# Attention and two mixtures of experts: the test for spilled tokens moved between expert 0's two products, the second tile's loads and splits rearranged, and zero products added in the first steps

## The chip, the cores and the metric

The kernel runs on one core of one Trainium2 chip. Times are device microseconds (us) of one execution of the whole program, less is better. Three executions are timed and a further one is profiled. The engines are PE (TensorE, matmul; PEld is its loading of weights), DVE (VectorE), ACT (ScalarE), POOL (GpSimd) and SP (SyncE, which here issues transfers). A "q" behind an engine's name means its instruction queue, which issues transfers, waits on semaphores, loads registers and branches.

## The reference

Sliding-window attention gives the rows of x; a mixture that sends each token to one of 8 experts follows, and then one that weighs 4 experts for every token.

```python
# 1. attention: B, H, S, D = 4, 8, 576, 64; window of 128 keys, a bias by distance and head
scores = np.where(mask, scale * q @ k.T + bias, -1e9); attn = softmax(scores)
x = (attn @ v).transpose(0, 2, 1, 3).reshape(2304, 512)
# 2. each token to its best of 8 experts (512 -> 1024 -> 512)
expert_idx = np.argmax(x @ w_gate, axis=1)
for e in range(8):
    xe = x[expert_idx == e]
    out[expert_idx == e] = gate_w * (np.maximum(xe @ w1[e], 0.0) @ w2[e])
# 3. four experts for all tokens, weighted by p
out2 += p[:, e:e+1] * (np.maximum(out @ w1[e], 0.0) @ w2[e])
```

## The kernel before

The order of the work is the order of the code: every engine runs its own instructions in the order in which they are written, and waits on semaphores for the others.

**Attention** (`attention()`) goes over 18 tiles of 128 tokens, each in two half steps s (four heads each), so 36 steps. A step runs on PE the scores of step s (`st_qk`, tile sc: first the bias by an identity in bf16, then products of q and k, each split into a high and a low part: qhi, qlo, khi, klo), the product with v of step s - 2 (`st_pv`, xo), for every second step the product of v with the gate (`st_vw`, vw) and the transposes of the probabilities of step s - 1 (`st_pv_t`, pt). DVE takes the row maximum (`st_max`, nm), which ACT's exponentials wait for, and makes the splits of a later tile (`split_k`, `split_q`). Tiles 0 and 1 are loaded and split ahead of the loop.

**First mixture** (`first_mixture()`): the rows of x lie sorted by expert in device memory (xs), 2304 places per expert. For each expert e the first 384 rows (CH) are fetched (`fetch`, tile row), transposed on PE (tile xps) and split by ACT (xhi) and DVE (xlo). `unit1(e)` is two products: the first, tile g, in four pairs of hidden blocks of 24 matmuls; after each pair ACT and DVE make hhi and hlo of it (`hidden`), PE transposes a quarter of the next expert's rows (`nprep`), and one tile of weights is split (`w_split`: ACT whi, DVE wlo, then SP's issue of the weights two tiles on, into one of three buffers raw). The second product, tile y, follows in four groups of 24 matmuls. The matmuls stand in arms of `by_width`, chosen by the expert's count of tokens. `prep_first` does expert 0's transposes at once, all four tiles.

**The test.** An expert with more than 384 tokens spills: `spill(e)` holds a loop over further chunks of 128. All of it stands in one `tc.If(most > 0)`, where `most` is read by every engine from nov_i. So each engine's queue loads the number, compares and jumps over the code of eight experts' loops. Behind the jump it waits for its own work and adds to its semaphores what the code that was jumped would have added. A tile that the spilled code also uses is so released for the next user only when the engine concerned has passed the test: the PSUM tiles of `ps_a` (tag a), for one, which ACT reads in the spilled code and y uses after it.

Line 869 ff. hold 24 zero products on PE ("idle"), which no one reads, between attention and the first mixture; then come two `w_split`, the test, `prep_first`, the fetch of expert 1's rows, and the eight `unit1`.

Of the kernel before, what the change touches and what calls it, by code (L numbers as in the profile page):

```python
# [45 lines left out]
def kernel(  # L46
# [42 lines left out]
    const.tile([P, PAD], F32, tag="pad", name="pad")  # L89


    stream = [(w_a, e, j) for e in range(E1) for j in range(NW)]
# [33 lines left out]
    def attention():  # L126
        actx = ExitStack()
        with actx:
# [16 lines left out]

            def load(t):
                rk = rpool.tile([P, NP, P], F32, tag="rk", name=f"rk{t}")
                rq = rpool.tile([P, NP, P], F32, tag="rq", name=f"rq{t}")
                nc.sync.dma_start(out=rk, in_=k[t])
                nc.sync.dma_start(out=rq, in_=q[t])  # L150
                raw_q[t], raw_k[t] = rq, rk
# [30 lines left out]
            nc.vector.memset(zrow, 0.0)  # L182
            load(0)
            wgt = c2.tile([P, NDT, E1], F32, tag="wgt", name="wgt")
            nc.sync.dma_start(out=wgt, in_=wg)
            load_v(0)
            load(1)
            load_v(1)
# [35 lines left out]
            for h in range(H):  # L224
                build_bias(0, h, 0, 2 * P, nc.scalar)
            split_k(1)
            split_q(1)
            dpt = c2.tile([P, N // P, E2], F32, tag="dpt", name="dpt")
# [303 lines left out]
            for s in range(ns + 2):  # L532
                t, hf = divmod(s, 2)
                if s < ns:
                    st_qk(s)
                    st_max(s)
                    st_exp(s, 0)
# [47 lines left out]
    def moe():  # L585
        mctx = ExitStack()
        with mctx:
# [57 lines left out]
            def first_mixture():  # L645
                pctx = ExitStack()
                with pctx:
# [77 lines left out]
                    def unit1(e, nprep, extra):  # L725
# [9 lines left out]
                        for f0 in range(0, NFT, 2):  # L735
                            pair = [ps_g.tile([P, CH], F32, tag="g", name="g") for _ in range(2)]

                            def body(w):
                                for r, ps in enumerate(pair):
                                    g1(ps, x, w0, f0 + r, w)  # L740

                            by_width(wide, pair, body)
                            hidden(pair, hs)
                            nprep(f0 // 2)
                            w_split()
                            extra()
                        accs = [ps_a.tile([P, CH], F32, tag="a", name=f"y{e}_{dt}") for dt in range(NDT)]
                        if e == E1 - 1:
# [22 lines left out]

                    def spill(e):
                        cur = sp.tile([P, 1], F32, tag="cur", name=f"cur{e}")
# [6 lines left out]
                        with tc.For_i(0, chunks_e, 1):  # L780
                            spill_chunk(e, cur, to)

                    def spill_chunk(e, cur, to):
                        ok = sp.tile([P, 1], F32, tag="ok", name="ok")
# [20 lines left out]
                        nc.vector.tensor_copy(out=xt, in_=px)  # L805
                        ht = xp.tile([P, NFT, P], F32, tag="xhi", name="sht")
                        raw = xp.tile([P, F], F32, tag="xlo", name="sraw")
                        for f in range(NFT):
                            if f % 2 == 0:
                                nc.sync.dma_start(out=raw, in_=w_a[e, f // 2])  # L810
                            ps = ps_g.tile([P, P], F32, tag="g", name="og")
                            for dt in range(NDT):
                                c0 = dt * 256 + (f % 2) * P
                                nc.tensor.matmul(
                                    ps, raw[:, c0:c0 + P], xt[:, dt, :], start=(dt == 0), stop=(dt == NDT - 1)
                                )
                            nc.scalar.activation(out=ht[:, f, :], in_=ps, func=AF.Relu)
                        accs = [ps_a.tile([P, P], F32, tag="a", name=f"oa{dt}") for dt in range(NDT)]
                        for f in range(NFT):
                            if f % 2 == 0:  # L820
                                nc.sync.dma_start(out=raw, in_=w_a[e, NW // 2 + f // 2])
                            for dt in range(NDT):
                                c0 = (f % 2) * DM + dt * P
                                nc.tensor.matmul(
                                    accs[dt], raw[:, c0:c0 + P], ht[:, f, :], start=(f == 0), stop=(f == NFT - 1)
                                )
# [41 lines left out]
                    rows = {0: fetch(0, ((0, 1), (1, 2), (2, 3)))}  # L868
                    ps = ps_g.tile([P, DM], F32, tag="g", name="idle")
                    for _ in range(24):  # L870
                        nc.tensor.matmul(ps, idle[:, 0:P], idle, start=True, stop=True)
                    for _ in range(2):
                        w_split()
                    most = nc.values_load(nov_i[0:1, E1:E1 + 1], min_val=0, max_val=NOV)
                    with tc.If(most > 0):
                        for e in range(E1):
                            spill(e)
                    prep_first(rows[0])
                    rows[1] = fetch(1, ((0, TT),))
# [138 lines left out]
```

## Time and profile before

| | |
|---|---|
| median of three timed runs | 1254.17 us (1251.94 to 1255.14) |
| profiled execution, its own time | 1245.32 us, span 1243.6 us |
| PE busy | 1219.8 us of the span (98%) |
| DVE, ACT, POOL busy | 528.3, 406.0, 86.5 us |
| granted PE clock, mean | 0.993 of full |

The span is first to last instruction of the profiled execution. What counts on this kernel is when PE has nothing to do or runs at half rate; the other engines' idle time alone costs nothing. The profiled execution is 8.9 us below the median of the timed ones.

### The profile page before, as it was taken

Reading aid. Unit: us, or ns where it says so; the run is one execution under the profiler, and the core shown is the slowest. Engines: PE = TensorE matmul, PEld = TensorE weight load, DVE = VectorE, ACT = ScalarE, POOL = GpSimd, SP = SyncE. Lnnn points to the kernel's source line nnn. Section 1 sums busy time; section 2 is a strip of 40 time slices with the busy share of each in tenths; the row PEclk is TensorE's granted clock in tenths of the full one; section 3 lists DMA queues with packets and bytes.
Section 4 is the critical chain, followed back from the end, with each engine's and each line's share of the span. In section 5 each row is a group of like instructions: output and inputs, shape, how many; then the busy total and the mean of one; then the engine's idle time right before and its main releaser. Section 6 shows DMA issues by size and latency. Waiting matters only on the chain.

```text
span 1243.6 us, 17916 instructions
## 1 busy us (share of the span) xinstructions
PE 1219.8 (98%) x7278; PEld 1117.7 (90%) x7278; DVE 528.3 (42%) x993; ACT 406.0 (33%) x777; POOL 86.5 (7%) x126
## 2 busy tenths in 40 slices
PE   8999998999999999999999999999999999999997
PEld 6888877999999999999999999999999999999996
DVE  5778764554555432342342242252253243234221
ACT  4565543454554331321231131141141132123110
POOL 8200110050000000000000000000000000000001
PEclk9999998999999999999999999999999999999999
DMA  8755414464564320120030040040030012011000
GB/s 286 266 158 183 145 69 166 142 202 156 170 194 147 117 69 1 51 85 1 21 115 1 1 135 1 26 161 26 1 103 33 1 53 83 1 34 51 26 14 38
DMA packets 57620, 109.87 MB, mean 88 GB/s; under 512 B 25760, under 2 KB 25760, under 8 KB 57504
## 3 DMA queue, kind: packets, MB, share of 16 engines
q1 hardware_dynamic: 54048, 98.71, 24.7%
q0 software_dynamic: 3456, 9.51, 2.0%
q8 instruction: 85, 1.39, 0.4%
q14 instruction: 31, 0.25, 0.1%
HBM read 92.40 MB, written 15.80 MB: 87 GB/s over the span
## 4 chain that ended last, share of the span: by engine, by line
PE 48%; issue 33%; POOL 1%; DVE 1%; DMA 0%; ACT 0%; POOLq 0%; SPq 0%; DVEq 0%
PE g L631 24%; PE a L941 14%; PE y L709 8%; PE y L720 1%; POOL out_dram L911 1%; PE xps L665 1%; DMA ct<-ctab 0%; DVE wlo L118 0%; PE g L690 0%; DVE acc L907 0%; POOLq L1014 0%; PE y L690 0%; DVE hlo L619 0%; ACT whi L114 0%; DVE xlo('s', 0)_4054 L610 0%
## 5 line engine op out<-in xcount | busy, mean ns | idle before, releaser
L619 DVE SCALAR_TENSOR_TENSOR hlo<-g,hhi 128x384 fp32r<-128x384 f32 x256 | 138.9, 555 | 519.8 <-ACT hhi L618 519.3
L618 ACT ACTIVATE hhi<-g 128x384 fp32r<-128x384 f32 x256 | 122.5, 491 | 620.6 <-PE g L631 576.3
L631 PE MATMUL g<-xhi,wlo 128*128 128x384 f32 x768 | 257.1, 335 | 0.0
L631 PE MATMUL g<-xhi,whi 128*128 128x384 f32 x768 | 257.0, 335 | 0.0
L631 PE MATMUL g<-xlo,whi 128*128 128x384 f32 x768 | 257.0, 335 | 0.0
L941 PE MATMUL a<-whi,hlo 128*128 128x512 f32 x576 | 224.7, 390 | 0.0
L941 PE MATMUL a<-wlo,hhi 128*128 128x512 f32 x576 | 224.6, 390 | 0.0
L941 PE MATMUL a<-whi,hhi 128*128 128x512 f32 x576 | 224.2, 389 | 0.0
L118 DVE TENSOR_TENSOR wlo<-raw,whi 128x1024 fp32r<-128x1024 f32 x128 | 154.7, 1224 | 107.3 <-ACT whi L114 107.1
L114 ACT CAST whi<-raw 128x1024 fp32r<-128x1024 f32 x128 | 133.0, 1059 | 52.4 <-DMA raw<-in_w_b_dram 28.4
L631 PEld LDWEIGHTS g<-xlo,whi 128*128 128x128 f32 x768 | 144.2, 188 | 1.1 <-DVE xlo L610 0.2
L631 PEld LDWEIGHTS g<-xhi,whi 128*128 128x128 f32 x768 | 144.2, 188 | 0.9
L631 PEld LDWEIGHTS g<-xhi,wlo 128*128 128x128 f32 x768 | 144.2, 188 | 0.0
L941 PEld LDWEIGHTS a<-whi,hlo 128*128 128x128 f32 x576 | 108.1, 188 | 22.5
L941 PEld LDWEIGHTS a<-wlo,hhi 128*128 128x128 f32 x576 | 108.2, 188 | 22.0
L941 PEld LDWEIGHTS a<-whi,hhi 128*128 128x128 f32 x576 | 108.2, 188 | 21.9
L911 POOL DMA_INDIRECT out_dram<-acc,ctok x18 | 17.8, 990 | 936.9 <-DVE acc L907 935.1
L360 ACT ACTIVATE pr<-sc,nm 128x256 f32<-128x256 f32 (+1 forms) x144 | 58.8, 465 | 56.0 <-DVE nm L352 32.8
L709 PE MATMUL y<-hhi,whi 128*128 128x256 f32 (+2 forms) x224 | 69.6, 311 | 1.7 <-issue 1.7
L386 PE MATMUL xo<-vr,ptr 128*128 128x73 f32 x544 | 70.6, 283 | 0.6 <-ACT ptr L373 0.5
L386 PEld LDWEIGHTS xo<-vr,ptr 128*128 128x128 f32 x544 | 65.1, 196 | 6.0 <-ACT ptr L373 1.3
L709 PE MATMUL y<-hhi,wlo 128*128 128x256 f32 (+2 forms) x224 | 69.0, 308 | 0.0
(201 smaller groups left out, 1411.2 us busy)
## 6 DMA issues: line engine op xcount, KB each, us to landing
raw<-in_w_a_dram SPq DMA_DIRECT2D x64, 512.0 KB, 4.3
raw<-in_w_b_dram SPq DMA_DIRECT2D x64, 512.0 KB, 3.6
xs<-zrow SPq DMA_DIRECT2D x8, 768.0 KB, 6.7
row<-xs SPq DMA_DIRECT2D x7, 768.0 KB, 5.5
rk<-in_k_dram SPq DMA_DIRECT2D x18, 256.0 KB, 5.1
rq<-in_q_dram SPq DMA_DIRECT2D x18, 256.0 KB, 5.3
vr<-in_v_dram SPq DMA_DIRECT2D x18, 256.0 KB, 3.9
rv<-in_vt_dram SPq DMA_DIRECT2D x18, 256.0 KB, 3.7
```

Source lines behind the costliest of these rows:

```text
L114: nc.scalar.copy(out=hi, in_=raw)
L118: nc.vector.tensor_tensor(out=lo, in0=raw, in1=hi.bitcast(F32), op=ALU.subtract)
L360: nc.scalar.activation(out=pr[:, r, jj, 0:w], in_=sc[s][:, r, jj, 0:w], func=AF.Exp, bias=nm[:, r, jj:jj + 1], scale=1.0,)
L386: nc.tensor.matmul(xo[:, 2 * jj + r, :], pt[:, r, c, :], vr[:, keys[c] % NSLOT, h, :], start=(c == 0), stop=(c == nk - 1),)
L618: nc.scalar.activation(out=hhi, in_=ps, func=AF.Relu)
L619: nc.vector.scalar_tensor_tensor(out=hlo, in0=ps, scalar=0.0, in1=hhi.bitcast(F32), op0=ALU.max, op1=ALU.subtract)
L631: nc.tensor.matmul(ps[:, 0:w], wl[:, c0:c0 + P], xl[:, dt, 0:w], start=(n == 0), stop=(n == 3 * NDT - 1),)
L665: nc.tensor.transpose(ps[:, t * P:(t + 1) * P], row[:, t, dt * P:(dt + 1) * P], ident)
L709: nc.tensor.matmul(acc[:, 0:w], wl[:, c0:c0 + P], hl[:, 0:w], start=(f == 0 and x == 0), stop=(f == NFT - 1 and x == 2),)
L720: nc.tensor.matmul(acc[:, 0:w], wl[:, c0:c0 + P], hl[:, 0:w], start=(f == 0 and x == 0), stop=(f == NFT - 1 and x == 2),)
L911: nc.gpsimd.indirect_dma_start(out=outv[g], out_offset=bass.IndirectOffsetOnAxis(ap=ctok[:, g, :], axis=0), in_=accs.pop(g), in_offset=Non ...
L941: nc.tensor.matmul(acc[t], hl[:, ts], wl[:, c0:c0 + DM], start=(f == 0 and n == 0), stop=(f == NFT - 1 and n == 2),)
```

## The change

Three things are moved or added. (1) In the first steps of attention, q of tiles 0 and 1 are loaded from ACT's queue in place of SP's, tile 1's loads go ahead of the gate weights and of v, and tile 1's splits are no longer ahead of the loop but at the start of step 2. (2) Zero products on PE (`busy`): nine ahead of the first scores, four after step 1's scores, three ahead of step 2's scores. (3) The test stands in `unit1(0)`, between the two products; `prep_first` follows the 24 zero products at once, ahead of the two `w_split`. The code of the spilled chunks takes its room from the pool of fetched rows (room) and loads its weights in smaller pieces.

```diff
+    def busy(pool, tag, n):
+        ps = pool.tile([P, DM], F32, tag=tag, name="idle")
+        for _ in range(n):
+            nc.tensor.matmul(ps, idle[:, 0:P], idle, start=True, stop=True)
...
-            def load(t):
+            def load(t, eng=nc.sync):
...
                 nc.sync.dma_start(out=rk, in_=k[t])
-                nc.sync.dma_start(out=rq, in_=q[t])
+                eng.dma_start(out=rq, in_=q[t])
...
-            load(0)
+            load(0, nc.scalar)
+            load(1, nc.scalar)
+            busy(ps_t, "t", 9)
             wgt = c2.tile([P, NDT, E1], F32, tag="wgt", name="wgt")
             nc.sync.dma_start(out=wgt, in_=wg)
             load_v(0)
-            load(1)
             load_v(1)
             load(2)
...
-            split_k(1)
-            split_q(1)
...
             for s in range(ns + 2):
                 t, hf = divmod(s, 2)
+                if s == 2:
+                    split_k(1)
+                    split_q(1)
+                    busy(ps_t, "t", 3)
                 if s < ns:
                     st_qk(s)
+                    if s == 1:
+                        busy(ps_t, "t", 4)
                     st_max(s)
                     st_exp(s, 0)
...
+                        if e == 0:
+                            most = nc.values_load(nov_i[0:1, E1:E1 + 1], min_val=0, max_val=NOV)
+                            room = rowp.tile([P, TT, DM], F32, tag="row", name="room")
+                            with tc.If(most > 0):
+                                for o in range(E1):
+                                    spill(o, room)
                         accs = [ps_a.tile([P, CH], F32, tag="a", name=f"y{e}_{dt}") for dt in range(NDT)]
...
-                        ht = xp.tile([P, NFT, P], F32, tag="xhi", name="sht")
-                        raw = xp.tile([P, F], F32, tag="xlo", name="sraw")
+                        ht = room[:, 0:2, :].rearrange("p a d -> p (a d)").rearrange("p (f c) -> p f c", c=P)
+                        raw = room[:, 2, :]
...
                     rows = {0: fetch(0, ((0, 1), (1, 2), (2, 3)))}
-                    ps = ps_g.tile([P, DM], F32, tag="g", name="idle")
-                    for _ in range(24):
-                        nc.tensor.matmul(ps, idle[:, 0:P], idle, start=True, stop=True)
+                    busy(ps_g, "g", 24)
+                    prep_first(rows[0])
                     for _ in range(2):
                         w_split()
-                    most = nc.values_load(nov_i[0:1, E1:E1 + 1], min_val=0, max_val=NOV)
-                    with tc.If(most > 0):
-                        for e in range(E1):
-                            spill(e)
-                    prep_first(rows[0])
                     rows[1] = fetch(1, ((0, TT),))
```

How this stands on the engines is shown at three places. The first is DVE's queue in the first steps, before (khi, klo, qhi, qlo are the splits, the third group of them tile 2's q; nm the maxima; vr receives vw):

```order
L173 TENSOR_SCALAR qhi_166<-rq_123 128x512
L174 SCALAR_TENSOR_TENSOR qlo_167<-rq_123,qhi_166 128x512
L164 CAST khi<-rk_131 128x4x128
L165 TENSOR_TENSOR klo<-rk_131,khi 128x4x128
L173 TENSOR_SCALAR qhi_180<-rq_132 128x512
L174 SCALAR_TENSOR_TENSOR qlo_181<-rq_132,qhi_180 128x512
L352 TENSOR_REDUCE nm_204<-sc_189 128x4
L352 TENSOR_REDUCE nm_237<-sc_222 128x4
L423 COPY vr<-vw_242 128x8x8
L173 TENSOR_SCALAR qhi_263<-rq_139 128x512
L174 SCALAR_TENSOR_TENSOR qlo_264<-rq_139,qhi_263 128x512
L352 TENSOR_REDUCE nm_290<-sc_275 128x4
```

And the same stretch of DVE's queue of the change (rq_149 is tile 2's q, rk_126 and rq_127 are tile 1's):

```order
L179 TENSOR_SCALAR qhi_176<-rq_123 128x512
L180 SCALAR_TENSOR_TENSOR qlo_177<-rq_123,qhi_176 128x512
L357 TENSOR_REDUCE nm_208<-sc_193 128x4
L357 TENSOR_REDUCE nm_246<-sc_226 128x4
L428 COPY vr<-vw_251 128x8x8
L179 TENSOR_SCALAR qhi_272<-rq_149 128x512
L180 SCALAR_TENSOR_TENSOR qlo_273<-rq_149,qhi_272 128x512
L170 CAST khi<-rk_126 128x4x128
L171 TENSOR_TENSOR klo<-rk_126,khi 128x4x128
L179 TENSOR_SCALAR qhi_286<-rq_127 128x512
L180 SCALAR_TENSOR_TENSOR qlo_287<-rq_127,qhi_286 128x512
L357 TENSOR_REDUCE nm_309<-sc_294 128x4
```

Tile 1's four splits have moved from ahead of the first two maxima to behind the splits of tile 2's q.

The second place is SP's queue between attention and the first mixture in the change (row_2768 and row_2835 are expert 0's and expert 1's rows, raw_2827 and raw_2833 the weights number 8 and 9):

```order
L668 DMA row_2768<-xs 128x512 x3
L109 DMA raw_2827<-in_w_a_dram 128x1024
L706 UNCONDITIONAL_BRANCH
L109 DMA raw_2833<-in_w_a_dram 128x1024
L668 DMA row_2835<-xs 128x3x512
```

The order of these transfers is the one of before, where the test stood between raw number 9 and expert 1's rows. What has moved is what raw number 9 waits for, the split wlo of weights 6 whose buffer it takes: on ACT that stretch now reads

```order
L620 CAST xhi('s', 0)_2797<-xps_0_2799 128x384
L620 CAST xhi('s', 0)_2797<-xps_1_2800 128x384
L620 CAST xhi('s', 0)_2797<-xps_2_2801 128x384
L620 CAST xhi('s', 0)_2797<-xps_3_2802 128x384
L120 CAST whi_2823<-raw_2085 128x1024
L120 CAST whi_2829<-raw_2418 128x1024
```

so the casts of weights 6 and 7 (raw_2085, raw_2418) have moved behind the four casts of expert 0's rows; before, they stood ahead of the test and of these.

The third place is ACT's queue at the end of expert 0's first product in the change:

```order
L629 ACTIVATE hhi<-g 128x384 x2
L620 CAST xhi('s', 1)_2945<-xps_3_3247 128x384
L120 CAST whi_3255<-raw_3057 128x1024
L761 TENSOR_LOAD nov_i
L763 COMPARE_AND_BRANCH
```

On PE the same test ends in these rows of the change, which name what an instruction waits for:

```order
L763 UNCONDITIONAL_BRANCH [waits PE_49,PE_sequencer_49]
L706 COMPARE_AND_BRANCH
L720 MATMUL y_0_4573<-hhi,whi_2003 128x384 [waits Activation_49]
L720 MATMUL y_0_4573<-hlo,whi_2003 128x384
L720 MATMUL y_0_4573<-hhi,wlo_2004 128x384
L720 MATMUL y_1_4574<-hhi,whi_2003 128x384 [waits Activation_49]
```

ACT's load and branch have moved behind the casts that follow the last pair, PE's stand ahead of its first y product, and this one waits for ACT's semaphore at a count that ACT reaches only with what it adds behind the test, since the spilled code would read the same PSUM tiles.

## Rows read from the trace of the kernel before

**Rows 1.** The page's costliest groups: busy us, mean ns of one, idle before.

```profile
L118 DVE TENSOR_TENSOR wlo<-raw,whi 128x1024 fp32r<-128x1024 f32 x128 | 154.7, 1224 | 107.3 <-ACT whi L114 107.1
L114 ACT CAST whi<-raw 128x1024 fp32r<-128x1024 f32 x128 | 133.0, 1059 | 52.4 <-DMA raw<-in_w_b_dram 28.4
```

**Rows 2.** PE's waits: us in total, times, longest us.

```profile
PE g L631 <- DVE xlo('s', 0)_4054 L610: 3.9, 1, 3.9
...
PE xps L675 <- PEq L875: 0.6, 1, 0.6
```

**Rows 3.** Timeline 183 to 205 us: start, us, instruction, idle before and releaser.

```profile
183.05 8.08 PE L871 MATMUL idle<-idle 128*128 128x512 bf16 x24
...
193.02 1.63 ACT L609 CAST xhi('s', 0)_4053<-xps 128x384 fp32r<-128x384 f32 x4 [3.77 <-DMA raw<-in_w_a_dram]
...
197.24 0.40 SPq L657 DMA_DIRECT2D row<-xs  x1
197.31 1.95 DVE L610 TENSOR_TENSOR xlo('s', 0)_4054<-xps,xhi('s', 0)_4053 128x384 fp32r<-128x384 f32 x4 [6.62 <-SPq L875]
...
204.03 0.49 PE L665 MATMUL xps<-ident,row 128*128 128x128 f32 x3
```

**Rows 4.** The test's load, L874: ns min/median/max, start in us.

```profile
L874 ACTq TENSOR_LOAD <-nov_i x1: 481/481/481, 187.2 to 187.2; - x1
L874 DVEq TENSOR_LOAD <-nov_i x1: 539/539/539, 189.3 to 189.3; - x1
```

**Rows 5.** The test's branch, L875: ns, first and last start in us.

```profile
L875 ACTq EVENT_SEMAPHORE  x2: 17/17/17, 190.5 to 190.6; - x2
...
L875 DVEq EVENT_SEMAPHORE  x2: 21/21/21, 194.7 to 194.8; - x2
```

**Rows 6.** Two stretches: length, busy us of each engine (instructions), granted clock, DMA share, GB/s.

```profile
190.00:195.00 5.00, 3.07 (x19) 1.77 (x16) 0.69 (x1) 1.63 (x4) 0.17 (x1) 1.00 0.81 305
198.00:202.00 4.00, 4.00 (x13) 4.00 (x14) 1.26 (x3) 0.00 (x0) 0.00 (x0) 0.50 0.89 300
```

**Rows 7.** Transfers issued at 197.2, 212.5, 244.9 us (rows), 6.8 us (q): KB, us to landing.

```profile
row<-xs SPq DMA_DIRECT2D x1, 768.0 KB, 4.4
...
row<-xs SPq DMA_DIRECT2D x1, 768.0 KB, 5.2
...
row<-xs SPq DMA_DIRECT2D x1, 768.0 KB, 7.2
...
rq<-in_q_dram SPq DMA_DIRECT2D x1, 256.0 KB, 5.2
```

**Rows 8.** Timeline at the end of expert 0's first product.

```profile
217.56 0.49 PE L665 MATMUL xps<-ident,row 128*128 128x128 f32 x3
...
217.80 0.42 PE L709 MATMUL y<-hhi,whi 128*128 128x384 f32 x1
...
218.70 3.11 ACT L114 CAST whi<-raw 128x1024 fp32r<-128x1024 f32 x3
```

**Rows 9.** Timeline of attention's first steps and, last three rows, of later ones.

```profile
8.23 0.43 DVE L164 CAST khi<-rk 128x512 fp32r<-128x512 f32 x1 [2.34 <-DMA rk<-in_k_dram]
...
9.00 1.89 PE L422 MATMUL vw<-wbd,rv 128*128 128x16 f32 x8
...
9.85 0.69 DVE L174 SCALAR_TENSOR_TENSOR qlo<-rq,qhi 128x512 fp32r<-128x512 f32 x1
...
11.95 0.43 DVE L173 TENSOR_SCALAR qhi<-rq 128x512 fp32r<-128x512 f32 x1
...
13.62 0.58 PE L343 MATMUL sc<-khi,qhi 64*128 64x256 f32 x2
...
31.40 0.39 PE L343 MATMUL sc<-khi,qhi 64*128 64x256 f32 x2
...
34.16 1.01 PE L422 MATMUL vw<-wbd,rv 128*128 128x16 f32 x8
...
40.59 0.39 PE L343 MATMUL sc<-khi,qhi 64*128 64x256 f32 x2
```

More of the change, by code (lines that the diff above doesn't have):

```diff
@@ L769, in unit1, with spill @@
                         extra()
-                    def spill(e):
+                    def spill(e, room):
                         cur = sp.tile([P, 1], F32, tag="cur", name=f"cur{e}")
@@ L780, in spill, with spill_chunk @@
                         with tc.For_i(0, chunks_e, 1):
-                            spill_chunk(e, cur, to)
-                    def spill_chunk(e, cur, to):
+                            spill_chunk(e, cur, to, room)
+                    def spill_chunk(e, cur, to, room):
                         ok = sp.tile([P, 1], F32, tag="ok", name="ok")
@@ L805, in spill_chunk @@
                         nc.vector.tensor_copy(out=xt, in_=px)
-                        ht = xp.tile([P, NFT, P], F32, tag="xhi", name="sht")
-                        raw = xp.tile([P, F], F32, tag="xlo", name="sraw")
+                        ht = room[:, 0:2, :].rearrange("p a d -> p (a d)").rearrange("p (f c) -> p f c", c=P)
+                        raw = room[:, 2, :]
                         for f in range(NFT):
-                            if f % 2 == 0:
-                                nc.sync.dma_start(out=raw, in_=w_a[e, f // 2])
+                            a0 = (f % 2) * P
+                            nc.sync.dma_start(
+                                out=raw.rearrange("p (d c) -> p d c", c=P),
+                                in_=w_a[e, f // 2].rearrange("p (d c) -> p d c", c=2 * P)[:, :, a0:a0 + P],
+                            )
                             ps = ps_g.tile([P, P], F32, tag="g", name="og")
                             for dt in range(NDT):
-                                c0 = dt * 256 + (f % 2) * P
                                 nc.tensor.matmul(
-                                    ps, raw[:, c0:c0 + P], xt[:, dt, :], start=(dt == 0), stop=(dt == NDT - 1)
+                                    ps, raw[:, dt * P:(dt + 1) * P], xt[:, dt, :], start=(dt == 0), stop=(dt == NDT - 1)
                                 )
@@ L819, in spill_chunk @@
                         for f in range(NFT):
-                            if f % 2 == 0:
-                                nc.sync.dma_start(out=raw, in_=w_a[e, NW // 2 + f // 2])
+                            d0 = (f % 2) * DM
+                            nc.sync.dma_start(out=raw, in_=w_a[e, NW // 2 + f // 2][:, d0:d0 + DM])
                             for dt in range(NDT):
-                                c0 = (f % 2) * DM + dt * P
                                 nc.tensor.matmul(
-                                    accs[dt], raw[:, c0:c0 + P], ht[:, f, :], start=(f == 0), stop=(f == NFT - 1)
+                                    accs[dt], raw[:, dt * P:(dt + 1) * P], ht[:, f, :], start=(f == 0), stop=(f == NFT - 1)
                                 )
```

## The prediction

> **What bounds the kernel now.** PE does, in nearly all of the span, so I looked for the places where it has nothing to do or runs slowly. The list of PE's waits comes first [rows 2]: its longest is 3.9 us, for expert 0's first xlo, and behind it stands a short one of 0.6 us for PE's own branch at the test. The timeline of that place shows how they hang together [rows 3]: the 24 zero products end at 183.05 + 8.08 = 191.13 us, ACT casts the transposed rows from 193.02, and DVE begins their xlo only at 197.31, after 6.62 us of idle time that an SP instruction of the test ended. The windows show the second loss [rows 6]: between 190 and 195 us PE is busy 3.07 of 5 us, and then, from 198 to 202 us, the granted clock is 0.50 (1.2 GHz) and PE issues 13 matmuls in 4.0 us. At the full 2.4 GHz the 72 matmuls and 9 transposes from 204.03 to 217.56 us [rows 3, 8] take 13.5 us, about 0.17 us each, so the 13 cost 4.0 - 2.2 = 1.8 us too much. The first steps of attention are slow as well: the eight vw products take 1.89 us at 9.00 and 1.01 us at 34.16, and three steps of scores, from 13.62 to 31.40, take 17.8 us where the next two take 9.2 [rows 9]. (The clock column reads 1.00 there too; the durations say half rate.)
>
> **The first steps.** Tile 1's four splits are taken from ahead of the first maxima: they run from 8.23 to 10.54 us now, 2.3 us of DVE [rows 9]. Their new place is behind the splits of tile 2's q. Those start at 11.95 us [rows 9], which is when their data lands: it is issued at 6.78 us and takes 5.2 [rows 7]. The transfers ahead of it are the same ones in another order, and they run back to back, so I leave 11.95. Then two q splits, half of 2.3 us, and khi, klo and qhi of tile 1, three quarters of 2.3: 11.95 + 1.15 + 1.7 = 14.8 us for the first scores of step 2, against 13.62. That is **+1.1 us**. The nine zero products at the start stand ahead of splits that PE waits for, and the last three in its wait for tile 1's. The four stand ahead of vw: at 8.08/24 = 0.34 us each [rows 3] vw would end at 9.0 + 1.4 + 1.9 = 12.3, and its copy, which is ahead of tile 2's q on DVE, would push that by 0.5 us; at full rate it would not. I take nothing and keep +0.5 as a bound. The two issues on ACT's queue fall ahead of the bias, under the same nine. What they may do to the clock is a rival below. In the forecast PE waits some 3 us for these splits and is as slow behind them as it was.
>
> **Expert 0's rows.** With the test gone, PE transposes at once (0.5 us earlier, about the 0.6 of [rows 2]), ACT's four casts run from 192.5 to 194.15 (1.63 us [rows 3]), and xlo follows cast by cast, to 194.9. The 24 matmuls of the first pair take 24 x 0.17 = 4.1 us, so PE is through at about 197.6, where it now is at 204.03. That would be 6.4 us. But the next thing in PE's queue is the transposition of expert 1's rows, and these are late next. SP issues them behind raw 9, raw 9 waits for wlo of weights 6, and ACT casts weights 6 after the four casts: 194.15 + 1.06 = 195.2, wlo to 196.45 [rows 1], raw 9 then, expert 1's rows 0.4 us (one issue [rows 3]) later, at 196.85. A fetch with a transfer of weights just ahead of it took 5.2 us [rows 7], so it lands at 202.05 and PE transposes then: **-2.0 us** against 204.03. The two bounds are 4.4 us (-2.8) and 7.2 us (0) [rows 7]; I take 5.2, since the rows at 212.5 have the same neighbour. PE stands still for 4.4 us, and after a stall of this kind the clock fell before [rows 3, 6]. The slow stretch that was paid ahead of 204.03 is paid after it: **+1.8 us**.
>
> **The test.** Its new place looks covered: y has all its weights, and DVE, SP and POOL can pass while PE works, so their share costs nothing (were DVE needed at once, it would be 5.5 us, below). ACT's share isn't covered, as the first y waits for it. The trace has the price: from ACT's load at 187.2 to the last of its two semaphore rows at 190.6 us, 3.4 us [rows 4, 5]. The load stands behind the cast that waits for the last transposes, 217.56 + 0.49 = 218.05 [rows 8]. So y could start at 218.05 + 3.4 = 221.5 instead of 217.80: **+3.7 us**. Below, it is bounded by whi, which ACT must have done: 218.70 + 1.06 = 219.8, +2.0. Above, by DVE's passing, 189.3 to 194.8: 5.5 us, y at 223.6, +5.8. I take ACT's own row.
>
> [...]
>
> The spilled code itself does not run (the trace has none of it), so its smaller loads and its room cost nothing.
>
> **Sum:** 1.1 - 2.0 + 1.8 + 3.7 = **+4.6 us**. On the profiled execution's own time that is 1245.3 + 4.6 = 1249.9. The timed runs lie 8.9 us higher, and I carry the difference over: 1254.2 + 4.6 = **1258.8 us**.
>
> **Rivals.**
>
> *The zero products hold the clock.* The 24 that stand behind attention were followed by the full clock at 190 us [rows 3, 6], so nine, four and three more may bring it up ahead of step 2. Three steps at the later pace would take 1.5 x 9.2 = 13.8 us instead of 17.8 [rows 9]. That is -4.0, and the term of the first steps becomes 1.1 - 4.0 = -2.9: sum +0.6, 1254.8 us, no change. If the timed runs are slow for two steps longer than the profiled one, it is another 2.7 us off, 1252. It decides whether PE's wait of about 3 us for tile 1's splits lets the clock fall again; against it speaks that it fell after the gaps between 191 and 195 us. [...]
>
> *Expert 1's rows are in time.* If they land by 197.6 us, PE does not stall and does not slow down: -6.4 in place of -2.0 + 1.8, sum 1.1 - 6.4 + 3.7 = -1.6, 1252.6 us. It needs a landing 4.4 us sooner than I work out, so raw 9 issued at once instead of behind wlo. Nothing in the order of the queues allows this, except that the end of attention shifts.
>
> *It gets worse.* ACT passes as slowly as DVE did (+2.1) and the clock falls a second time, at the test (+1.8): sum 8.5, 1262.7 us. A stall of 3.7 us is near to the one after which it fell.
>
> **Chances and range.** The forecast 0.45, the zero products 0.22, the rows in time 0.12, worse 0.21. A difference under 0.3% (3.8 us) can't be told from none on this kernel. The forecast's own bounds (+0.5 of the first steps, -0.8 to +2.0 of the fetch, -1.7 to +2.1 of the test) give +2.1 to +9.2, two thirds of it over 3.8; with "worse" that is about 0.50 slower. Same takes the rest of the forecast and most of the two rivals, 0.37. Faster is 0.13: a rival that comes together with another, or the longer slow stretch. The range holds the forecast's bounds and reaches to the middle of the first two rivals and to "worse": 1250 to 1264.
>
> **What would show it.** In the changed kernel's timeline: step 2's first scores about 1 us later, and vw of step 3 still at 1.9 us; a wait of PE for expert 1's rows of some 4 us after the first pair, with the clock at 0.5 behind it; a wait of PE for ACT or its own branch of 3 to 4 us ahead of the first y. The prediction is wrong if vw stands at 1.0 us from tile 1 on, if xps of expert 1 starts right behind the first pair, or if y follows the last transposes within 1 us.

## The result, and the profile of the changed kernel

The change makes the kernel slower. Four executions took 1264.84 to 1270.25 us, median 1267.11; the kernel before took 1251.94 to 1256.85, median 1254.66, beside them. The ratio is 1.0102 (95% interval 1.0072 to 1.0132), and the medians are 12.4 us apart. The profiled execution took 1264.84 us, its span is 1262.9 us against 1243.6, its mean granted clock 0.985 against 0.993. The spans differ by 19.3 us, the times by 12.4, since the profile of before lies 9 us under its timed executions and that of the change only 2 us.

The first view is again the list of PE's waits (us in total, times, longest).

```profile
PE xps L676 <- DMA row<-xs: 6.2, 1, 6.2
PE g L642 <- DVE hlo L630: 6.0, 2, 3.7
PE g L642 <- remote: 4.7, 1, 4.7
PE y L720 <- ACTq L763: 3.8, 1, 3.8
```

Before, PE had none of them but a wait of 0.6 us for hlo. The first and the last were forecast; the two in the middle were not. They lie in expert 2's first product (3.7 of the 6.0 us for hlo, and all of the 4.7) and in expert 4's (the other 2.3 us for hlo). The timeline of the changed kernel shows each place (start, us, instruction, idle before and its releaser).

```profile
9.22 0.96 PE L427 MATMUL vw<-wbd,rv 128*128 128x16 f32 x8
...
13.71 0.39 PE L348 MATMUL sc<-khi,qhi 64*128 64x256 f32 x2 [1.57 <-DVE qhi L179]
...
20.46 1.01 PE L427 MATMUL vw<-wbd,rv 128*128 128x16 f32 x8
...
191.92 0.92 SPq L668 DMA_DIRECT2D row<-xs  x1
...
199.36 0.90 PE L676 MATMUL xps<-ident,row 128*128 128x128 f32 x3 [6.24 <-DMA row<-xs]
...
214.83 0.49 PE L676 MATMUL xps<-ident,row 128*128 128x128 f32 x3
219.10 0.45 PE L720 MATMUL y<-hhi,whi 128*128 128x384 f32 x1 [3.78 <-ACTq L763]
...
272.34 0.49 ACT L629 ACTIVATE hhi<-g 128x384 fp32r<-128x384 f32 x1 [7.21 <-remote]
...
286.64 0.87 ACT L629 ACTIVATE hhi<-g 128x384 fp32r<-128x384 f32 x2 [9.31 <-remote]
```

Read it beside [rows 9], [rows 3] and [rows 8]. The eight vw products take 0.96 us from the first tile on (1.89 before), so PE runs at the full rate in most of the first steps; from 16 to 19 us it is at half rate once more (granted clock 0.50, 17 matmuls in 3.0 us). Expert 1's rows are issued at 191.92 and PE has them at 199.36. y starts 4.27 us behind the start of the last transposes, where 0.24 us lay between them before. And in expert 2, ACT twice stands idle for 7 to 9 us ahead of a g whose products PE had already done. ("Remote" means that no instruction of the trace is seen to send the signal that ended the wait.)

The third view is the test itself in the changed kernel (its load, line 761, and its branch, line 763: ns min/median/max, first and last start in us).

```profile
L761 ACTq TENSOR_LOAD <-nov_i x1: 282/282/282, 215.4 to 215.4; - x1
...
L763 PEldq EVENT_SEMAPHORE  x2: 51/51/51, 218.3 to 218.5; - x2
L763 ACTq EVENT_SEMAPHORE  x2: 17/17/17, 219.0 to 219.1; - x2
L763 DVEq EVENT_SEMAPHORE  x2: 21/21/21, 221.2 to 221.3; - x2
...
L763 PEldq COMPARE_BRANCH  x1: 5433/5433/5433, 212.8 to 212.8; - x1
```

PE's branch stands in its queue for 5.4 us, and PE is through at 218.5, half a microsecond ahead of ACT. In the kernel before PE's branch took 3.6 us, while the zero products ran until 191.13:

```profile
L875 PEldq COMPARE_BRANCH  x1: 3552/3552/3552, 186.2 to 186.2; - x1
```

The fourth view is the clock (length, PE busy and instructions, the other engines, granted clock, DMA share, GB/s).

```profile
199.50:203.50 4.00, 4.00 (x14) 4.00 (x15) 1.78 (x2) 1.42 (x2) 0.00 (x0) 0.50 0.04 14
...
220.60:224.00 3.40, 3.40 (x12) 3.40 (x12) 2.36 (x2) 0.60 (x1) 0.00 (x0) 0.50 0.67 180
...
266.00:270.00 4.00, 2.90 (x21) 2.48 (x19) 0.39 (x1) 0.00 (x0) 3.18 (x3) 1.00 0.48 134
270.00:274.00 4.00, 0.43 (x1) 0.46 (x2) 0.97 (x2) 0.98 (x2) 3.00 (x4) 0.72 0.03 3
...
282.00:286.00 4.00, 1.20 (x3) 0.58 (x2) 0.00 (x0) 0.00 (x0) 1.94 (x2) 0.50 0.03 3
```

Behind each of the two waits PE is at half rate, as it was in [rows 6]. From 266 to 286 us DVE, ACT and the transfers do little, PE stands still for about half of the time, and only POOL is busy until 284.5 (it scatters the places by 18 small indirect transfers).

The timelines give a table of stages: how much longer each took than in the kernel before, first for the two profiles above, then for two pairs of profiles taken later (below). The first stage is all from the start to PE's last count of experts (tile rkp), which ends at 183.19 us before and 179.01 after.

| stage, up to | first pair | second pair | third pair |
|---|---|---|---|
| last count of experts | -4.2 | -1.1 | -0.2 |
| expert 1's rows transposed (xps) | -0.5 | +0.4 | -0.2 |
| last xps of that product | +1.9 | +1.6 | +2.0 |
| y of expert 0 | +4.0 | +3.9 | +4.0 |
| g of expert 1 | +1.6 | +2.4 | 0.0 |
| y of expert 2 | +16.9 | 0.0 | 0.0 |
| g of expert 5 | +0.8 | +2.6 | -1.1 |
| end of the span | -1.2 | -1.2 | -1.2 |
| sum | +19.3 | +8.7 | +3.3 |

### The profile page after: what moved, and what is told of

Its sections match the earlier page's. It is cut to its first block, busy times and chain, and to the rows that moved or that the text cites. A ratio compares the mean times of both kernels' runs of the same rounds, so it can differ in the third digit from the quotient of the medians.

```text
span 1262.9 us, 17945 instructions
## 1 busy us (share of the span) xinstructions
PE 1223.0 (97%) x7292; PEld 1118.0 (89%) x7294; DVE 528.7 (42%) x993; ACT 406.2 (32%) x777; POOL 86.3 (7%) x126
## 4 chain that ended last, share of the span: by engine, by line
PE 43%; issue 35%; another core or an unknown queue 2%; POOL 1%; DMA 0%; ACT 0%; DVE 0%; POOLq 0%; SPq 0%; ACTq 0%
PE g L642 20%; PE a L955 13%; PE y L720 8%; PE y L731 1%; POOL out_dram L925 1%; PE xps L676 1%; DMA ct<-ctab 0%; ACT whi L120 0%; PE g L701 0%; DVE acc L921 0%; DVE hlo L630 0%; ACT hhi L629 0%; PE y L701 0%; DVE wlo L124 0%
## 5 line engine op out<-in xcount | busy, mean ns | idle before, releaser
L720 PE MATMUL y<-hlo,whi 128*128 128x256 f32 (+2 forms) x224 | 69.4, 310 | 0.0
```

Source lines behind the costliest of these rows:

```text
L720: nc.tensor.matmul(acc[:, 0:w], wl[:, c0:c0 + P], hl[:, 0:w], start=(f == 0 and x == 0), stop=(f == NFT - 1 and x == 2),)
```

## The experiments

All ratios are to the kernel before, timed beside each kernel; it took 1239 to 1240 us (median) in all four later comparisons, each of them on a chip of its own, 15 us less than in the first. Differences in us are between medians, unless said otherwise.

**The change in two halves.** The kernel before with the first steps of the change:

```diff
-            load(0)
+            load(0, nc.scalar)
+            load(1, nc.scalar)
+            busy(ps_t, "t", 9)
...
-            split_k(1)
-            split_q(1)
...
+                if s == 2:
+                    split_k(1)
+                    split_q(1)
+                    busy(ps_t, "t", 3)
...
+                    if s == 1:
+                        busy(ps_t, "t", 4)
```

> The first steps as in the change (loads, splits, zero products), the test and everything behind attention as before. In the profile of the change attention ends at 175.8 us where before it ended at 180.0, and 16.4 us are lost between 266 and 292 us, in expert 2's first product. Theory 1, the loss at expert 2 belongs to the moved test: this kernel does not have it and is 4 us under before's profile, span near 1239 to 1240. Theory 2, the loss belongs to the earlier end of attention or comes by chance: it shows here too, span near 1255. In both, vw of tile 1 takes about 1.0 us and the first scores of step 2 stand near 13.7 us.

Measured: ratio 0.9995 (0.998 to 1.001), nothing. No loss at expert 2. And the test alone, which is the change with the first steps of before (the edit is against the change):

```diff
-            load(0, nc.scalar)
-            load(1, nc.scalar)
-            busy(ps_t, "t", 9)
+            load(0)
...
+            split_k(1)
+            split_q(1)
...
-                if s == 2:
-                    split_k(1)
-                    split_q(1)
-                    busy(ps_t, "t", 3)
...
-                    if s == 1:
-                        busy(ps_t, "t", 4)
```

> The moved test with all that goes with it (transposes of expert 0's rows ahead of the two splits of weights, room from the pool of fetched rows), but loads, splits and zero products of the first steps as before. Theory 1, the loss at expert 2 belongs to the moved test: it shows here, some 16 us, and the span is near 1243.6 + 7 + 16 = 1267. Theory 2, chance or the shifted time: the loss is absent, span near 1243.6 + 7 = 1250. The 7 are what the profile of the change shows from attention's end to expert 1: rows 0.7 us less, slow pair 1.9, wait ahead of y 4.0, slow stretch in y 1.6.

Measured: ratio 1.0063 (1.0046 to 1.008), 8.4 us. No loss at expert 2 here either: the theory that ties it to the moved test fell. The waits are those of the change: 6.6 us for expert 1's rows, 3.7 us for ACT ahead of y. So the slowdown that can be repeated belongs to the third part of the change, the test with the order of the work around it.

**The scattering of the places later.**

```diff
-                        unit1(e, nprep, lambda e=e: e > 0 and next(post, None))
+                        unit1(e, nprep, lambda e=e: e > 2 and next(post, None))
```

> The change, with the scattering of the places (18 indirect transfers of POOL, which run from 260.8 to 284.5 us in the profile of the change) begun in expert 3 in place of expert 1. Theory 1, PE's signals are held up by these transfers: the loss at expert 2 is gone, span near 1247; it may come back as a loss in experts 3 to 5 beside the transfers' new place. Theory 2, the loss is a late consequence of the jump alone (code of the engines behind it): it stays between 266 and 292 us, span near 1263.

Measured: ratio 1.0043 (1.003 to 1.0056), span 1245.5 us. There was no loss at expert 2, but since the change itself did not have one in its later runs either (next), this run tells nothing of it.

**The change again, twice.**

> The change itself once more. On another chip the first steps alone, the test alone, and the change with late places showed no loss at expert 2. Theory 1, the loss of 16.4 us at expert 2 belongs to this kernel wherever it runs: it is there, and the ratio is 1.010 or more. Theory 2, it belongs to one chip or to chance: it is absent, and the ratio is near that of the change with late places, 1.004 to 1.006, which the steps from attention's end to expert 1 explain (7 us of 1240 is 0.0056).

> The change a third time. In its first profile 16.4 us were lost in expert 2's first product, in the second none. Theory 1, the loss belongs to the first chip or to its state: if this chip takes 1240 us for the kernel before, there is no loss and the ratio is 1.006 to 1.008 again; if it takes 1254, the loss is there and the ratio near 1.010. Theory 2, it comes by chance in single executions: it may show here at the same time of the kernel before, and the times of this kernel spread by over 10 us.

Measured: 1.0068 (1.0047 to 1.0089), 9.4 us, and 1.0080 (1.0062 to 1.0099), 8.5 us. No loss at expert 2 in either profile, spans 1248.0 and 1242.6 us (the latter is the fastest of its executions). So the loss does not come with this kernel wherever it runs; what it is stays open. **The kernel before again, twice**, for profiles beside these:

> The kernel before, for a second profile. In the first one PE's clock came up at 28.2 us of the span and attention ended at 180.0; the test alone, which leaves the first steps as they are here, had it up at 15.0 and attention ended at 174.2. Theory A, when the clock comes up in the first steps is not set by these steps alone and differs between executions: attention ends anywhere between 174 and 180 us here. Theory B, it is fixed for this kernel: 180 again.

> The kernel before a third time, for its profile on this chip. Theory 1, as for the run of the change beside it: on a chip that takes 1254 us for it there are losses in its first mixture too, of some 10 us, with PE's signals seen several us late; on one that takes 1240 there are none.

Measured: ratios 1.0005 (0.9987 to 1.0022) and 1.0011 (0.9991 to 1.0032), as it should be. Theory A held: the counts of experts end at 180.0 and 178.9 us here against 183.2 in the first profile, with the same code. These are the second and third pair of the table. They show two places where kernels differ from execution to execution. One is y of expert 0. In the second profile of the change the clock falls in it,

```profile
219.00:223.90 4.90, 4.90 (x16) 4.90 (x17) 2.28 (x2) 1.97 (x2) 0.00 (x0) 0.50 0.42 121
...
343.50:346.80 3.30, 3.30 (x19) 3.21 (x18) 2.32 (x4) 1.85 (x4) 0.00 (x0) 0.50 0.57 181
```

and in the third it doesn't (30 matmuls in the 4.9 us in place of 16):

```profile
219.00:223.90 4.90, 4.90 (x30) 4.90 (x29) 2.36 (x2) 2.69 (x3) 0.00 (x0) 1.00 0.52 151
```

Of the ten profiles of kernels here with a wait of 3.4 to 3.8 us ahead of y, eight have a half-rate stretch in y, of 3.4 or 6.8 us, which makes the product 1.3 to 2.7 us longer than the 16.9 us that it takes without. In the seven profiles without such a wait y takes the 16.9 us every time. The other place is expert 4, at 340 us. There DVE's copy of the token numbers (ctok) waits for a transfer of 72 KB, with the last pair's hlo behind it in DVE's queue. DVE's waits in that stretch of the second profile of the change:

```profile
DVE ctok L885 <- DMA ct<-ctab: 3.1, 1, 3.1
```

and of the second profile of before:

```profile
DVE ctok L865 <- DMA ct<-ctab: 1.5, 1, 1.5
```

The transfer took 5.8 and 4.1 us. The longer one made PE wait 2.2 us for hlo and put it at half rate behind that (the row of 343.50 above).

**Expert 1's rows fetched earlier**, in the change:

```diff
                     rows = {0: fetch(0, ((0, 1), (1, 2), (2, 3)))}
+                    rows[1] = fetch(1, ((0, TT),))
                     busy(ps_g, "g", 24)
```

> The change, with the fetch of expert 1's rows issued right behind expert 0's, ahead of the weights. Theory, the rows are late because SP issues them behind raw 9: the wait of 6.2 us after the first pair and the half clock behind it (1.9 us) go, 8 us less up to y; expert 0's own rows may land up to 3 us later since the queue shares its engines. The wait ahead of y stays 3 to 4 us. The loss at expert 2 stays if it belongs to the test and its distance from the scattering of the places, so the span would be near 1255 to 1258. Rival, the fetch takes 7 us wherever it is issued because the weights run beside it: no change.

Measured: ratio 1.0013 (0.9997 to 1.0029), against 1.0068 of the change: 0.0055 less, 6.8 us of the 8 expected. The wait for the rows is gone, the transposes stand at 192.73 us, right behind the first pair; the slow stretch is gone too. The wait ahead of y, 3.6 us, and the half rate in y stayed. Expert 0's own rows were in time: the list of PE's waits, which goes down to 0.2 us, has none for them. So the rows' place behind the weights was the cause. That it was raw 9's wait, as the prediction said, the timeline of the change shows (raw 8 and 9 in one row, both wlo in one):

```profile
183.97 7.91 SPq L109 DMA_DIRECT2D raw<-in_w_a_dram  x2
...
190.29 2.36 DVE L124 TENSOR_TENSOR wlo<-raw,whi 128x1024 fp32r<-128x1024 f32 x2
```

Between raw 8 and raw 9 SP waits 7.1 us for the first wlo, which ends near 191.5 us; then raw 9 goes out, and the rows follow at 191.92.

**The spilled chunks' accumulators in another pool**, so that y no longer waits for ACT's passing; alone, and together with the early rows:

```diff
-                        accs = [ps_a.tile([P, P], F32, tag="a", name=f"oa{dt}") for dt in range(NDT)]
+                        oacc = ps_g.tile([P, NDT, P], F32, tag="g", name="oa")
+                        accs = [oacc[:, dt, :] for dt in range(NDT)]
```

> The change, with the spilled chunks' accumulators in a tile of the pool of g in place of the pool that y uses, so that y's first product no longer waits for ACT behind the test. Theory, ACT's passing is the whole price of the test's new place: the wait of 3.8 us ahead of y goes, and the slow stretch in y (1.6 us) with it, 5.4 us less than the change; the first g of expert 1 waits for nothing, since ACT has passed 15 us earlier. Rival, PE's own passing of the test is as slow as ACT's: a wait of 2 us or more ahead of y stays, with PE's own queue as its releaser.

> Both remedies on the change: expert 1's rows fetched right behind expert 0's, and the spilled chunks' accumulators in the pool of g. If both theories hold, PE has no wait over 1 us and no half clock from attention's end to expert 1, and the kernel is faster than before: 10 us for the place where the test stood (PE idle or slow from 190 to 204 us in before) less 1 to 2 for the casts, so 4 to 8 us under before, ratio 0.994 to 0.997. Rival, the clock falls somewhere else and takes 2 us back: ratio 0.997 to 1.000.

Measured: 1.0068 (1.0045 to 1.0091) alone, as the change; 1.0012 (0.9994 to 1.0029) together, as with early rows alone. The theory fell and the rival held. PE's waits in the first of the two kernels:

```profile
PE xps L676 <- DMA row<-xs: 6.6, 1, 6.6
PE y L720 <- PEq L763: 3.4, 1, 3.4
```

The wait has only changed its name: PE's own queue now releases y, 3.4 us late. PE is through nearly as late as ACT.

**The change without the test.**

```diff
-                        if e == 0:
-                            most = nc.values_load(nov_i[0:1, E1:E1 + 1], min_val=0, max_val=NOV)
...
-                            with tc.If(most > 0):
-                                for o in range(E1):
-                                    spill(o, room)
```

> The change without the test and without the code of the spilled chunks (no expert's spilled tokens would be computed; with these inputs there are none). Theory, the wait of 3.9 us ahead of y and the slow stretch of 2.4 us in y are the test's: both go, and with them the later loss at expert 4 may change by its distance from the clock; 6 us under the change on the same chip, ratio near 1.002 to 1.003 to before. Rival, the slow stretch in y comes from the wait for expert 1's rows and would fall in any case: 3.9 us only, 1.004.

Measured: 1.0037 (1.0023 to 1.0051), 0.0031 and 0.0043 below the two ratios of the change, which is 4 to 5 us. The kernel is still slower than before: the wait for expert 1's rows (4.4 us here) and the slow stretch behind it are left. Of this kernel's clock (same columns as above):

```profile
196.00:202.00 6.00, 3.70 (x13) 3.70 (x14) 1.78 (x2) 1.42 (x2) 0.00 (x0) 0.50 0.46 176
214.00:224.00 10.00, 10.00 (x61) 10.00 (x60) 5.36 (x7) 5.17 (x7) 0.00 (x0) 1.00 0.62 206
```

y starts 0.25 us behind the last transposes and runs at full rate, while the slow stretch behind the wait for the rows is still there. So each of the two waits had a slow stretch of its own, and the one in y goes with the test: eight of the ten profiles with the wait have it, none of the seven without.

**The change without the first steps' zero products** (the 9, 4 and 3):

```diff
-            busy(ps_t, "t", 9)
...
-                    busy(ps_t, "t", 3)
...
-                    if s == 1:
-                        busy(ps_t, "t", 4)
```

> The change without the 9, 4 and 3 zero products of the first steps. Theory A, they hold the clock: without them attention ends near 180 us, as in the first profile of before, and the kernel is 4 us slower than the change, ratio 1.010. Theory B, the clock comes up near 15 to 20 us in any case, and nothing changes on average: attention ends between 174 and 180, ratio 1.005 to 1.008.

Measured: 1.0080 (1.0056 to 1.0103), no different from the change. The last count of experts ends at 180.6 us. Over all these later profiles it ends at 179.0 us in the mean of nine with the change's first steps (177.5 to 180.3), and at 178.5 in the mean of five with those of before (177.4 to 180.0). The mean is that of the first steps as a whole. No gain by the zero products is seen, in the time or there; one of 1 us would not be seen.

**The copy of the token numbers a step later**, in the change:

```diff
                         nc.sync.dma_start(out=ct, in_=ctab.rearrange("(c p) k -> p c k", p=P))
+                        yield
```

> The change, with DVE's copy of the token numbers one step (a pair of products, 3.2 us) behind the transfer ct that it waits for. In the profile of the change on this chip DVE waits 5.8 us for it, PE 2.2 us for hlo, and the clock is at half for 3.4 us behind that, from 343 to 347 us; on the first chip the wait was there too. Theory, this loss of 2.5 us belongs to that copy: it goes, ratio near 1.005 in place of 1.007. Rival, another transfer or split is late there: the wait stays.

Measured: 1.0057 (1.0036 to 1.0079). (Of the 5.8 us of the transfer DVE had waited 3.1, as shown above.) The wait for hlo at expert 4 is gone from the profile, and a shorter one, of 1.0 us, stands in expert 4's y; the gain is too small against the interval to be shown by the time.

**The test in its old place, but first there.** In the kernel before, the test ahead of the splits of weights, expert 1's rows early, and the copy later:

```diff
                     rows = {0: fetch(0, ((0, 1), (1, 2), (2, 3)))}
+                    rows[1] = fetch(1, ((0, TT),))
...
-                    for _ in range(2):
-                        w_split()
                     most = nc.values_load(nov_i[0:1, E1:E1 + 1], min_val=0, max_val=NOV)
...
                     prep_first(rows[0])
-                    rows[1] = fetch(1, ((0, TT),))
+                    for _ in range(2):
+                        w_split()
```

> The kernel before, with the test in its old place but ahead of the two splits of weights, which follow the casts of expert 0's rows; expert 1's rows fetched right behind expert 0's; DVE's copy of the token numbers one step behind the transfer that it waits for. First steps as before. Theory, in the old place PE and ACT pass the test under the 24 zero products, and only SP (5.5 us from its load) and DVE pass late, since their loads stand behind the weights: now they pass near 190.5 us in place of 193.8, xlo follows at once, PE has no wait of 3 us and no half clock in the first pair, expert 1's rows are there. y near 208.5 us in place of 214.0 (second profile of before), 5 to 6 us faster, ratio 0.995 to 0.996. Rival, the splits of weights, now later, make raw 8 and 9 late and the time is lost at y: ratio 0.998 to 1.000.

Measured: 0.9992 (0.9979 to 1.0004). y starts at 212.1 us, not at 208.5. The test's line in this kernel (line 875) shows why:

```profile
L875 SPq EVENT_SEMAPHORE  x9: 17/17/17, 190.5 to 191.4; - x9
...
L875 DVEq EVENT_SEMAPHORE  x2: 21/21/21, 188.1 to 188.2; - x2
```

And DVE's first xlo:

```profile
191.52 1.95 DVE L610 TENSOR_TENSOR xlo('s', 0)_4044<-xps,xhi('s', 0)_4043 128x384 fp32r<-128x384 f32 x4 [7.61 <-ACT whi L114]
```

DVE is through at 188.2, but xlo starts at 191.52, behind SP's last semaphore: the spilled weights would be loaded into the buffer that xlo takes. (The row names ACT's whi as the releaser, whose first cast ends at about the same time; the next run leaves these casts where they are and settles it.) So, last, with a tile of its own for them, and the smaller loads of the change:

```diff
-                        raw = xp.tile([P, F], F32, tag="xlo", name="sraw")
+                        raw = sp.tile([P, DM], F32, tag="sraw", name="sraw")
```

> As the kernel with the test first (test ahead of the weights in its old place, expert 1's rows early, token numbers copied a step later), with the spilled chunks' weights in a tile of their own in place of the buffer of xlo. In the profile of the kernel with the test first SP passed at 190.5 to 191.4 us and DVE's xlo started at 191.5, two us after the casts, and the clock was at half from 189.9 to 196.8 us. Theory, SP's passing is all that held xlo: it starts with the casts near 189.5, PE's wait of 1.8 us and most of the slow stretch go, y near 208 us in place of 212.1, ratio 0.995 to 0.997 to before. Rival, DVE or the casts wait for something else there and the clock falls anyway: ratio 0.999.

Measured: 0.9948 (0.9934 to 0.9962), 1232.39 us against 1239.25: faster than both kernels. y starts at 207.5 us. Its clock from the zero products to y:

```profile
182.80:187.70 4.90, 3.97 (x24) 2.21 (x22) 0.00 (x0) 0.48 (x2) 0.22 (x1) 1.00 0.90 298
187.70:193.90 6.20, 5.00 (x26) 4.39 (x27) 4.31 (x6) 3.19 (x6) 0.00 (x0) 1.00 0.49 141
193.90:207.50 13.60, 13.60 (x85) 13.50 (x83) 8.14 (x12) 6.64 (x13) 0.00 (x0) 1.00 0.60 195
```

The test's last row on SP, and xlo:

```profile
L876 SPq EVENT_SEMAPHORE  x9: 17/17/17, 189.1 to 189.7; - x9
...
187.73 1.95 DVE L610 TENSOR_TENSOR xlo('s', 0)_4108<-xps,xhi('s', 0)_4107 128x384 fp32r<-128x384 f32 x4 [5.39 <-ACT xhi('s', 0)_4107 L609]
```

SP passes this test at 189.7 us, 2 us after xlo has begun, and no wait in the lists of PE, DVE and ACT names it. The clock does not fall. Not all of the gain lies here: of the 9.0 us between this profile and the third of before, 1.6 lie ahead of the last count of experts, 3.9 from there to y, and 3.5 behind y, where the copy of the token numbers also differs.

## Why the prediction was right and wrong

The sign was right, the size was not: I forecast +4.6 us, and the medians were 12.4 us apart in the comparison that counts, 9.4 and 8.5 in the two later ones.

**The first steps (+1.1).** The place was right: step 2's first scores wait for tile 1's qhi. But they start at 13.71 us, 0.1 later than before, not 1.1 (14.8 less 13.62 is 1.2, by its own figures): tile 2's q, for which I had left 11.95, is split from 10.65 us on, 1.3 us sooner (it is issued at 6.32 us in place of 6.78). And PE was not as slow behind them as it had been. In the first pair of profiles it looks as if the rival held, zero products that bring the clock up (-4.2 us). The later runs take that back: with the first steps of before PE came to the full rate for good at 28 us in the first profile and between 15 and 21 us in the five others, and the first steps alone gave a ratio of 0.9995 (0.998 to 1.001), neither loss nor gain. I had read a property of the kernel from one execution.

**Expert 0's rows (-2.0).** PE did stand still for expert 1's rows, and for the reason given (the early fetch showed it). But the fetch took 7.4 us in the profile and 6.8 and 7.1 later, in place of the 5.2 that I took. This is near my own upper bound, 7.2 [rows 7], at which the gain is nothing, and nothing is about what was measured (-0.5, +0.4, -0.2). So this term was mis-sized by some 2 us in all three pairs.

**The half clock behind it (+1.8)** was right: +1.9, +1.6, +2.0. (PE's pace at the two clocks, in the trace of before: zero products of 512 columns start every 426 ns at 0.50, 11 in 4.69 us from 183.43 on, and every 216 ns at 1.00, 9 in 1.94 us from 188.81 on. That is 1.2 and 2.4 columns per ns, and the prediction's two figures in GHz are shown as these rates alone.)

**The test (+3.7)** was right in size: +4.0, +3.9, +4.0. ACT needed 3.7 us from its load at 215.4 to its last semaphore, where its rows of before gave 3.4. (ACT's branch by itself lasts 45 ns in the trace; the time lies behind it.) The reasoning was incomplete, though: "ACT's share isn't covered" is true, but PE's own share isn't covered either. Its branch took 3.6 us under the zero products before and 5.4 us here, and I had looked for ACT's and DVE's rows only. With y freed of ACT a wait of 3.4 us stayed. That PE is through only 0.6 us ahead of ACT is luck: had it been slower, ACT's row would have given the wrong size.

**The step that failed**, in the comparison that counts, is a term that the sum put at nothing: what happens behind y. In the first pair the sum's own stages, up to the end of expert 0's y, gave -4.2 - 0.5 + 1.9 + 4.0 + 1.6 = +2.8 us, less than forecast; 16.9 of the 19.3 us were lost in expert 2. I had looked at no stage behind y, and the cause of this loss stays open (below). In the later pairs, where it is absent, two steps of the sum itself fail. One is the -2.0 of expert 0's rows, which came to nothing. The other is that the sum lets the clock fall once: the stall of 3.7 us ahead of y brought a second slow stretch in eight of ten profiles (+1.6 and +2.4 us in two of three pairs). I had this in the rival "it gets worse" with 0.21, beside an ACT that passes as slowly as DVE, which it did not. With what was measured in the second pair the same terms give -1.1 + 0.4 + 1.6 + 3.9 + 2.4 = +7.2. The rest of its 8.7 comes from the stages behind, above all +2.6 up to expert 5, where PE waits for expert 4's hlo behind the copy of the token numbers. In the third pair the clock did not fall in y, and the two profiles differ by only 3.3 us.

**The loss at expert 2** was there in one of the change's three profiles, and in none of the other fourteen. In it PE's matmuls stand in the trace in time, but ACT gets their signal 5.7 and 9.1 us later, while POOL scatters the places. The same scattering at the same place disturbs nothing in the later profiles. It need not be the chance of one execution: all four executions of the change in that comparison took 1264.84 us or more, where its later ones took 1244.60 to 1251.20, and those of the kernel before took 1251.94 or more, where later ones took 1235.95 to 1245.65. So I suspect that in that comparison both kernels lost time in this way, the one before too in its timed executions (its profiled one took 1245.32), and that the 12.4 us are some 9 of the change and a difference in these losses. No trace shows that. Whether the chip, its state at that time or something else made the difference was not tested, and the cause stays open.

## What to carry to other kernels

A test that every engine must pass cost each engine 3 to 7 us here, though nothing of what it guards was done. It held PE up for no more than 0.6 us only in the last kernel, where it stood under the zero products and the fetch of expert 0's rows, and where none of its tiles was needed next. Look in the trace for the row of the jump on every engine, the covered ones too, before it is moved. Price a stall of some 4 us on PE together with the half-rate stretch behind it (here 3.4 or 6.8 us at a clock of 0.50, with 21 of 23 stalls), and don't take the clock's course of one execution for the kernel's.

## What the runs showed of the hardware

Between the end of attention and expert 1, PE stood still for 3.2 to 6.6 us in 23 places of the seventeen profiles (for xlo, for expert 1's rows, ahead of y), and with 21 of these stalls the granted clock fell to half, for 3.4 or 6.8 us each time, part of it within the stall in some; yet the third profile of the change and that of the test alone passed the wait of 3.7 us ahead of y at full rate. With zero products at the start PE came to the full rate near 5 us in eight profiles of ten, but in seven of these it fell back to half for 3 to 7 us between 8 and 20 us, as in this row of the first steps alone:

```profile
16.00:20.00 4.00, 4.00 (x25) 2.88 (x24) 2.76 (x8) 2.10 (x6) 3.72 (x7) 0.57 1.05 403
```

The engines differ in how long they need to pass the same test. In the kernel with the test first PE's branch took 3.6 us (from 181.6), and the first semaphore row behind the branch came 4.4 us after the load on DVE (183.7), 3.3 on ACT (182.9) and 5.3 on SP (185.2). A transfer of 72 KB in packets of 32 bytes (ct, 2304 rows of 8 numbers) took 4.0 to 5.8 us in these profiles, as long as one of 512 KB of weights (median 4.3 in the kernel before).
